# Decision thresholds that vary along the program, in a list schedule that is made at build time

## The chip, the cores and the metric

One core of one Trainium2 chip. The metric is the device time of one execution in microseconds (us). PE is TensorE, ACT ScalarE, DVE VectorE, POOL GpSimd, SP the engine that issues most DMAs. "Before" and "after" are the two kernels. A profile's span is some 1.5 to 2 us shorter than the device time of the same execution.

## The reference

```python
# x: 2048 tokens x 512, bf16; 32 heads of 16; F = 1376
def reference(x, wqkv, wo, w1, b1, w2, b2):
    xn = layernorm(x)
    # A: q, k, v = split(xn @ wqkv); p = softmax(q @ k.T * 16 ** -0.5); A = (p @ v) @ wo
    # B: a token mixer: h = layernorm(xn); u = gelu(h.T @ w1 + b1); B = (u @ w2 + b2).T
    return x + A + B
```

The cost is the softmax: 32 heads of 2048 x 2048 scores have to go through an exponential.

## The kernel before

The work is cut into 1024 score tiles of 128 x 1024, each made by two matmuls and kept in one of three PSUM slots. Its exponential is taken in one of two ways: on ACT, with one instruction; or on DVE, as integer arithmetic on the bits of a bf16 number, with three shifted copies on DVE or POOL that PE then sums up. A tile on ACT gives one PV item (four matmuls) to PE, a tile on DVE four.

The program holds no loop on the chip. At build time a scheduler in the kernel's own Python keeps a clock for each engine, asks again and again which job could start first, and appends that job to its engine's list. Six thresholds steer the choices:

```python
SEG = 8
RULES = (            # D_LATE, D_BACK, D_STEAL, PAIR_WAIT, piece_min, LATE_BY
    (0.5, 0.5, 0.3, 0.0, 6, 0),
    (0.3, 0.5, 0.3, 0.0, 6, 0),
    (0.8, 0.5, 0.3, 0.0, 4, 0),
    (0.5, 0.8, 0.3, 0.0, 6, 0),
    (0.5, 0.5, 0.45, 0.15, 6, 0),
    (0.5, 0.5, 0.15, 0.0, 4, 0),
    (0.5, 0.35, 0.3, 0.3, 4, 0),
    (0.8, 0.8, 0.3, 0.0, 99, 0),
    (0.5, 0.5, 0.3, 0.0, 4, 6),
    (0.5, 0.8, 0.45, 0.1, 4, -6),
)
RULE_OF = "000...0"                       # 128 digits, all 0
...
while True:                               # next_n: the score tile to come, 32 to 1023
    D_LATE, D_BACK, D_STEAL, PAIR_WAIT, piece_min, LATE_BY = RULES[int(RULE_OF[min(next_n, NN - 1) // SEG])]
    ...
    # may DVE take tile n?
        if qi == 0 and len(ready_q) == 1:
            if act_free - t < D_STEAL:    # ACT is about to take it
                continue
        if backlog(t) > D_BACK:           # DVE has too much waiting
            continue
    ...
    # PE: which job; is other work so late that it goes first; when are scores wanted; wait to pair two?
    jobs.append((max(t_c, est(...)), 1 if late > -LATE_BY else 3, "ext", cur_ext, 0.214))
    ...
    wants.append(sc.free["dve"] + backlog(sc.free["dve"]) + D_LATE)
    ...
    go = max(e_s, t2 if t2 <= need + PAIR_WAIT else need)
    ...
    # (piece_min: how many steps of other work must be left to place one, in four pieces, beside scores)
```

PE works in two layouts that alternate. A score phase has matmuls on 32 rows each ("S": one tile on half the array, two tiles on all of it; a piece of other work can fill a free quarter). A column phase has matmuls on 32 columns each ("C": PV items and steps of projections and of the mixer, the "other work"). The instructions that the argument touches:

```python
e.matmul(bank(bk), lhsT=KT[32*r:32*r+32, T, 128*kt:128*(kt+1)], rhs=QT[32*r:32*r+32, b % 4, :], ...)       # L776 scores
e.activation(buf(pbuf[n]), ps[:, s_*1024:(s_+1)*1024], ACTF.Exp, scale=LN2_128)                            # L800 exponential on ACT
e.tensor_scalar(buf_i(w), ps[:, s_*1024:(s_+1)*1024], IBIAS, 0.0, ALU.add, ALU.max)                        # L811 exponential on DVE
e.int64_add(buf_i(o)...)  /  e.tensor_scalar(buf_i(o), buf_i(w), float(SHIFTS[k]), 1.0, ALU.add, ALU.mult) # L817 POOL / L820 DVE: a shift
e.matmul(bank(PV_BANK)[32*c:32*c+32, 256*par:256*par+256], lhsT=vt[:, off:off+32], rhs=buf(p, ...), ...)    # L843 PV
e.matmul(bank(EX_BANK)..., tile_position=(0, 32*c)) / (..., tile_position=(32*r, 0))                        # L874 / L882 other work: step / piece
```

The softmax here doesn't subtract the row's maximum and nothing guards it: scores larger than these inputs give would overflow.

## Time and profile before

| | before |
|---|---|
| time, median of 4 runs | 689.69 us (689.63 to 689.81) |
| span of the profile | 688.0 us |
| exponentials on ACT / on DVE | 712 / 312 |
| shifts on POOL / on DVE | 643 / 293 |
| shortest spacing of ACT's exponentials | 0.903 us |
| score phases on PE (from 45 us) | 655 |

The counts come from the page's groups, which show an instruction's shape and number; where one kind has several groups (tile names pT and x_sb) they are added. The spacing and the phases are read from the start times in the trace.

### The profile page before, as it was taken

The page shows a single profiled execution, that of the slowest core. Times are in us where ns is not written, and L with a number is a line of the kernel's source. Part 1 is how long each engine was busy: PE and PEld are TensorE (multiplying, and loading weights), DVE is VectorE, ACT ScalarE, POOL GpSimd, SP SyncE. Part 2 cuts the span into 40 slices and gives each one's busy share as a digit, 9 for nine tenths or more (in the row PEclk, how much of TensorE's full clock was granted, in tenths as well). Part 3 has the DMA queues.
Part 4 walks back from the last instruction along what each step waited for, and adds up shares of the span by engine and source line. Part 5 has one row for each costly group of instructions (what it writes and reads, how often), then busy time and mean ns, then how long its engine had stood idle before and what let it go on. Part 6 is the DMA issues. An engine that isn't in the chain of part 4 may idle for free.

```text
span 688.0 us, 29503 instructions
## 1 busy us (share of the span) xinstructions
PE 674.2 (98%) x12966; PEld 310.9 (45%) x12966; DVE 620.9 (90%) x893; ACT 669.4 (97%) x732; POOL 407.9 (59%) x702
## 2 busy tenths in 40 slices
PE   8999999999999999999999999999999999999998
PEld 4534554445544454444444444444444444444444
DVE  7989899988899989999999999999999889889986
ACT  6999999999999999999999999999999999999994
POOL 5546557555566545766476576765666566555652
PEclk9999999999999999999999999999999999999999
DMA  7502100221002200122220112222221222212121
GB/s 215 132 7 52 27 16 19 51 46 25 20 19 51 47 20 20 32 44 44 52 42 21 40 46 56 53 56 55 49 60 25 57 54 56 62 42 65 40 50 44
DMA packets 86256, 32.85 MB, mean 48 GB/s; under 512 B 67440, under 2 KB 86128, under 8 KB 86128
## 3 DMA queue, kind: packets, MB, share of 16 engines
q1 hardware_dynamic: 85696, 30.58, 19.0%
q8 instruction: 101, 1.65, 1.0%
q10 hardware_dynamic: 432, 0.39, 0.2%
q14 instruction: 27, 0.22, 0.1%
HBM read 21.76 MB, written 2.35 MB: 35 GB/s over the span
## 4 chain that ended last, share of the span: by engine, by line
PE 60%; ACT 34%; DVE 3%; issue 1%; POOL 1%; DMA 0%; DVEq 0%
PE ps L843 25%; ACT pT L800 23%; PE ps L776 22%; PE ps L874 11%; ACT x_sb L800 10%; PE ps L928 1%; ACT gT_sb L985 1%; DVE pT L811 1%; DVE hx L588 1%; POOL mv L584 0%; DVE OT L1062 0%; DMA x_sb<-in_A_x_dram 0%; PE ps L669 0%; DVE x_sb L811 0%; PE ps L600 0%
## 5 line engine op out<-in xcount | busy, mean ns | idle before, releaser
L800 ACT ACTIVATE pT<-ps 128x1024 bf16<-128x1024 f32 x513 | 502.6, 1122 | 2.8 <-PE ps L776 2.1
L811 DVE TENSOR_SCALAR pT<-ps 128x1024 int16<-128x1024 f32 x229 | 279.6, 1221 | 22.7 <-PE ps L776 16.2
L776 PE MATMUL ps<-QT,KT 32*128 32x512 bf16 x2048 | 284.2, 384 | 6.3 <-ACT pT L800 2.6
L817 POOL INT64_ADD pT<-pT x339 | 205.0, 613 | 115.9 <-DVE pT L820 68.3
L843 PE MATMUL ps<-pT,V 128*32 128x256 bf16 x4732 | 245.4, 275 | 1.8 <-DVE OT L1062 1.3
L800 ACT ACTIVATE x_sb<-ps 128x1024 bf16<-128x1024 f32 x199 | 213.9, 1130 | 0.3 <-PE ps L776 0.2
L776 PEld LDWEIGHTS ps<-QT,KT 32*128 32x128 bf16 x2048 | 78.2, 91 | 183.2 <-ACT pT L800 71.9
L843 PEld LDWEIGHTS ps<-pT,V 128*32 128x32 bf16 x4732 | 111.7, 96 | 74.8 <-issue 59.3
L817 POOL INT64_ADD x_sb<-pT x135 | 82.2, 612 | 68.0 <-DVE pT L820 32.0
L843 PE MATMUL ps<-x_sb,V 128*32 128x256 bf16 x1860 | 117.8, 275 | 0.0
L811 DVE TENSOR_SCALAR x_sb<-ps 128x1024 int16<-128x1024 f32 x83 | 101.4, 1221 | 9.2 <-PE ps L776 6.6
L817 POOL INT64_ADD pT<-x_sb x118 | 71.4, 614 | 43.3 <-DVE pT L820 21.9
L820 DVE TENSOR_SCALAR pT<-pT 128x1024 int16<-128x1024 int16 x149 | 63.1, 427 | 4.4
L843 PE MATMUL ps<-pT,VM 128*32 128x256 bf16 x896 | 63.0, 275 | 0.0
L874 PE MATMUL ps<-gT_sb,wblk 128*32 128x512 bf16 (+1 forms) x704 | 60.2, 383 | 0.0
L843 PEld LDWEIGHTS ps<-x_sb,V 128*32 128x32 bf16 x1860 | 47.4, 96 | 27.7 <-issue 20.8
L874 PE MATMUL ps<-hx,wblk 128*32 128x512 bf16 x598 | 52.3, 383 | 0.0
L817 POOL INT64_ADD x_sb<-x_sb x51 | 31.1, 614 | 18.0 <-DVE pT L820 10.7
L882 PE MATMUL ps<-hx,wblk 32*128 32x512 bf16 (+1 forms) x92 | 35.6, 387 | 0.0
L843 PEld LDWEIGHTS ps<-pT,VM 128*32 128x32 bf16 x896 | 23.9, 96 | 12.9 <-issue 11.7
L820 DVE TENSOR_SCALAR x_sb<-pT 128x1024 int16<-128x1024 int16 x64 | 27.3, 428 | 2.0
L820 DVE TENSOR_SCALAR pT<-x_sb 128x1024 int16<-128x1024 int16 x59 | 25.2, 429 | 1.5
(107 smaller groups left out, 452.3 us busy)
## 6 DMA issues: line engine op xcount, KB each, us to landing
wblk<-in_B_w_dram SPq DMA_DIRECT2D x10, 512.0 KB, 4.2
wblk<-in_B_w_dram SPq DMA_DIRECT2D x16, 320.0 KB, 3.6
oC<-OT SPq DMA_DIRECT2D x248, 16.0 KB, 1.8
denb<-rden_scratch SPq DMA_DIRECT2D x124, 32.0 KB, 2.1
xr<-in_A_x_dram SPq DMA_DIRECT2D x16, 128.0 KB, 2.7
dcomp<-OT SPq DMA_DIRECT2D x124, 2.0 KB, 2.3
QT<-Qall SPq DMA_DIRECT2D x120, 16.0 KB, 1.8
out_dram<-osb SPq DMA_DIRECT2D x14, 128.0 KB, 1.9
```

The costliest lines, as they stand in the source:

```text
L588: return [dict(eng="dve", fn=lambda e: e.tensor_scalar(xn_sb[:, t, :], xn_sb[:, t, :], mv[:, t, 3:4], None, ALU.mult), reads=[("xn", t), ( ...
L776: specs.append(dict(eng="pe", fn=lambda e, r=r, bk=bk: e.matmul(bank(bk), lhsT=KT[32 * r:32 * r + 32, T, 128 * kt:128 * (kt + 1)], rhs=QT[ ...
L800: return [dict(eng="act", fn=lambda e: e.activation(buf(pbuf[n]), ps[:, s_ * 1024:(s_ + 1) * 1024], ACTF.Exp, scale=LN2_128), reads=[("ban ...
L811: return dict(eng="dve", fn=lambda e: e.tensor_scalar(buf_i(w), ps[:, s_ * 1024:(s_ + 1) * 1024], IBIAS, 0.0, ALU.add, ALU.max), reads=[(" ...
L817: return dict(eng=eng, fn=lambda e: e.int64_add(buf_i(o).bitcast(I64), buf_i(w).bitcast(I64), SHIFTS[k] * 0x0001000100010001), reads=[("pT ...
L820: return dict(eng=eng, fn=lambda e: e.tensor_scalar(buf_i(o), buf_i(w), float(SHIFTS[k]), 1.0, ALU.add, ALU.mult), reads=[("pT", w)], writ ...
L843: specs.append(dict(eng="pe", fn=lambda e, c=c, h=h, i=i, off=off: e.matmul(bank(PV_BANK)[32 * c:32 * c + 32, 256 * par:256 * par + 256], ...
L874: specs.append(dict(eng="pe", fn=lambda e, c=c, w=w: e.matmul(bank(EX_BANK)[32 * c:32 * c + w, :], lhsT=lhs_of(32 * c, 32 * c + w), rhs=rh ...
L882: return [dict(eng="pe", fn=lambda e: e.matmul(bank(EX_BANK)[0:dst_rows, :], lhsT=lhs_of(0, dst_rows)[rs], rhs=rhs[rs], start=begin, stop= ...
L928: return [dict(eng="pe", fn=lambda e, ct=ct, c=c: e.matmul(bank(EX_BANK)[32 * c:32 * c + 32, 128 * i:128 * (i + 1)], lhsT=xnT[:, ct, 128 * ...
L985: yield "act", [dict(eng="act", fn=lambda e, ap=ap: e.activation(ap, ap, ACTF.Gelu_apprx_tanh), reads=[("gT", f) for f in fts], writes=[(" ...
```

## The change

Its intent, as the change describes itself: let the thresholds differ along the program, with a new entry for every eight score tiles, found by a search whose replay of the lists has late DMAs and PE's clock. Of the search only its result is in the kernel.

```diff
-RULE_OF = "00000000000000000000000000000000000000000000000000000000000000000000000000000000000000000000000000000000000000000000000000000000"
+RULE_OF = "00008220310000100058660800426859400150020974970367941473943140809177076731670813606801617338009600085119008766223163090020510000"
```

## The prediction

> **What bounds the kernel now.** I read the page first, then the waits of ACT and DVE, the windows, and one timeline in detail.
>
> The page's first, second and fourth part:
>
> ```profile
> PE 674.2 (98%) x12966; PEld 310.9 (45%) x12966; DVE 620.9 (90%) x893; ACT 669.4 (97%) x732; POOL 407.9 (59%) x702
> ...
> PEclk9999999999999999999999999999999999999999
> ...
> PE 60%; ACT 34%; DVE 3%; issue 1%; POOL 1%; DMA 0%; DVEq 0%
> ```
>
> Two engines are nearly full and the chain of waits hops between them (PE 60%, ACT 34%); DMA is not on it. The clock row is full everywhere, so there is no clock to win.
>
> The waits of ACT, then of DVE:
>
> ```profile
> ACT oT L1162 <- PE ps L1155: 7.4, 1, 7.4
> ACT xnT L594 <- PE ps L600: 2.9, 3, 1.4
> ACT pT L800 <- PE ps L776: 2.1, 6, 0.5
> ...
> DVE pT L811 <- PE ps L776: 16.2, 69, 0.5
> DVE x_sb L811 <- PE ps L776: 6.6, 25, 0.5
> ```
>
> ACT's large waits are one in the tail and a few at the start; inside the stream its exponentials show 2.1 us of waiting. DVE waits 16.2 + 6.6 = 22.8 us for score tiles.
>
> The windows, cut where the table begins to act (about 45 us) and where the exponentials end (677 us):
>
> ```profile
> 0.00:45.00 45.00, 39.55 (x444) 19.93 (x444) 37.05 (x109) 38.28 (x46) 21.58 (x59) 1.00 0.50 133
> 45.00:677.00 632.00, 626.90 (x12418) 286.73 (x12420) 578.14 (x773) 630.22 (x686) 386.34 (x644) 1.00 0.18 42
> 677.00:688.00 11.00, 7.71 (x114) 4.28 (x106) 5.74 (x13) 0.95 (x2) 0.00 (x0) 1.00 0.14 48
> ```
>
> Only the middle 632 us can move; the 45 + 11 = 56 us around them are issued by code that doesn't consult the table. In the middle ACT is covered for 630.22 of 632 us and PE for 626.90.
>
> One stretch of the timeline (start, duration, instruction, count):
>
> ```profile
> 202.72 0.39 PE L776 MATMUL ps<-QT,KT 32*128 32x512 bf16 x2
> 202.73 0.39 PE L882 MATMUL ps<-hx,wblk 32*128 32x512 bf16 x1
> ...
> 203.04 0.40 PE L843 MATMUL ps<-pT,V 128*32 128x256 bf16 x8
> ...
> 203.15 1.18 ACT L800 ACTIVATE x_sb<-ps 128x1024 bf16<-128x1024 f32 x1
> ...
> 203.49 0.39 PE L776 MATMUL ps<-QT,KT 32*128 32x512 bf16 x4
> ...
> 203.81 0.40 PE L843 MATMUL ps<-pT,V 128*32 128x256 bf16 x8
> ...
> 204.07 1.18 ACT L800 ACTIVATE pT<-ps 128x1024 bf16<-128x1024 f32 x1
> ...
> 204.97 1.19 ACT L800 ACTIVATE x_sb<-ps 128x1024 bf16<-128x1024 f32 x1
> ```
>
> An exponential is recorded as 1.18 us, but the next starts 0.90 to 0.92 us later: work must be counted by starts. A score phase on PE takes 0.32 us whether it holds one score tile (two matmuls, here with one piece of other work beside them: 202.72 to 203.04) or two (four matmuls: 203.49 to 203.81). The phase between has three PV items of four matmuls: 203.04 to 203.49, 0.45 us.
>
> **What the Trainium skill says.** "Perfetto Trace Analysis", section "Per-instruction lifecycle", has the recorded window of a DVE or ACT instruction run to the acknowledged write, and calls PE's recorded end an estimate; so busy shares overstate how full these engines are. The trace agrees (1.18 recorded against 0.90 to 0.92 between starts). "ScalarE: Activation LUTs", section "What ACT_TABLE_LOAD costs", gives 186 ns + 0.833 ns an element for an ACTIVATE with immediate operands, with an overlap of 93 ns: 1039 - 93 = 946 ns between starts for 1024 elements. The trace has 903 ns at the shortest, and the trace decides. "TensorE: Matmul & The Clock Gate", Part 3, "The mechanism", says that matmuls on different row groups overlap; the equal 0.32 us for one and two score tiles agrees. "SBUF — State Buffer", section "SBUF: two separate sides", has DVE (in its two-port modes) and GpSimd exclude each other on a shared port pair; POOL's many waits for DVE's shifts (L820) fit that, though part of them is the program's own ordering.
>
> **The change part by part.** Only the string that names one of ten rules for each eight score tiles changes. No instruction kind is added; the order changes, and with it (a) which tiles go to DVE, (b) which of a tile's three shifts go to DVE or POOL, (c) how scores pair on PE. Of 128 entries the first four aren't consulted (32 tiles are issued before); of the other 124, 86 leave rule 0. Entries with a larger permitted DVE backlog (rules 3, 7, 9): 30; with scores wanted earlier for DVE (rule 1): 14; with an earlier takeover by DVE (rule 5): 5; with a later one (4, 9): 16; waiting to pair scores (4, 6, 9): 29. A mixture, with a lean to more tiles on DVE, and found by a search whose aim was the end time.
>
> ACT. The trace has 712 exponentials on ACT and 312 on DVE (of 1024). At 0.903 us between starts, 712 x 0.903 = 643 us. From the first start (11.4 us) to the last end (677.3 us) are 666 us. GELU with two table loads takes 398.13 to 406.10, about 8 us. What is left is 666 - 643 - 8 = 15 us, of which I read about 2 us in the fixed first part: some 13 us in the stream, most of it in pieces of 0.02 us. I give the search a third: **4 us**. Anything beyond that must come from exponentials leaving ACT: 0.90 us each.
>
> DVE. Between 45 and 677 us its start-to-start times add up to 632: 383 after the 311 exponentials (L811), 155 after the 292 shifts (L820), 93 for the rest. So one tile costs DVE (383 + 155)/311 = 1.73 us. The shortest spacings (1.135 and 0.342) would make it 1.135 + 0.94 x 0.342 = 1.46 us; the difference is the 22.8 us of waiting for scores, some 31 us in which a shift waits for its own exponential (1.258 against 1.131 us, 248 times), and what port and order cost. If the span shrinks by x, DVE has 538 - x us for 312 + (x - 4)/0.90 tiles:
> - x = 8: 316.4 tiles, 1.675 us each, 0.05 us less than now, or about 17 us of stalls gone;
> - x = 13.8 (2%): 322.9 tiles, 1.62 us each, about 0.10 us less, or 34 us of stalls gone, more than every recorded wait for scores.
> The first asks for less than all the recorded waits for scores; the second needs a second source, such as shifts given to POOL, which is busy only 59%.
>
> PE. In the middle it runs 655 score phases (322 of two tiles, 123 of one, 202 of one with a piece, 8 others) and 656 column phases; the score phases take 230 us and the column phases 401. A column phase takes about 0.118 us plus 0.1085 for each PV item plus 0.2165 for each step of other work; over that and 0.32 for a score phase only some 14 us of the 631 are left. A tile moved to DVE brings three more PV items, 3 x 0.1085 = 0.33 us. For x = 8 with four more tiles PE must lose 8 + 1.4 = 9.4 us: say 5 of the 14 us excess, and 4.4 from ten fewer pairs of phases (0.32 + 0.118 = 0.44 us each; 1.5% of 655). For x = 13.8 with eleven more it must lose 17 us: 5, and 27 pairs of phases, while every pairing that removes a half-empty score phase also removes a place for a piece.
>
> Sum: 4 us of ACT gaps + 4 to 5 exponentials off ACT (4 us) = 8 us.
>
> **The rivals.** First, the search overfits its model: the order fits modelled starts, and small differences on the chip turn into in-order waits. For it: both engines are so tight that 0.02 us slips are spread over the exponentials. Against: PE's longest recorded wait for ACT is 0.4 us, so the existing list's model fits well, and late DMAs were modelled in the search. Time then: 686 to 690. Second, the search finds the second source (POOL takes shifts, DVE takes ten or more tiles, PE pairs more): 672 to 676. For it: POOL's 41% of idle time, 322 paired phases out of a possible 512, and eighty-six entries to choose. Against: three engines have to give way together, and thresholds only nudge a greedy choice that already takes the earliest job. Third, the clock: gaps on PE could lower it; with PE this full I see no room for that, so no cost and no gain.
>
> **Range and chances.** The middle estimate is 689.65 - 8.2, about 681.5 us (-1.2%). The range 675.5 to 687 holds from two thirds of the second rival's gain to most of the first's loss. Faster by over 2% means under about 676: 0.13. Slower by over 2% would take 14 us of new waits in an order selected for its end time: 0.01. The rest, 0.86, lies within 2%.
>
> **What would show it.** DVE's exponentials at 314 to 320 instead of 312, ACT's at 704 to 710; the sum of ACT's gaps in the stream down from 13 to about 9 us; DVE's waits for scores well under 22.8 us; score phases about 645 instead of 655; head and tail as before; the same clock. If the count on DVE stays at 312 and the time still falls, the gain is gaps alone. I am wrong if over ten tiles move to DVE (then over 2%), if ACT gains nothing, or if POOL takes clearly more shifts than 643.

## The result, and the profile after

| | before | after |
|---|---|---|
| time, median (4 runs each) | 689.69 us | 685.26 us (684.96 to 685.32) |
| ratio, 95% interval | | 0.9935 (0.9917 to 0.9952) |
| span of the profile | 688.0 us | 683.2 us |
| exponentials on ACT / on DVE | 712 / 312 | 711 / 313 |
| shifts on POOL / on DVE | 643 / 293 | 658 / 281 |
| score phases on PE from 45 us | 655 | 652 |

Ratios here are the mean time of one kernel's fast runs over that of the other's of the same rounds, so not quite the ratio of the medians. The time fell by 4.43 us, 0.65%: within 2%, inside the range of the prediction, and about half of its middle estimate.

The page of after, the same three lines as in the prediction:

```profile
PE 671.5 (98%) x12975; PEld 312.9 (46%) x12978; DVE 617.0 (90%) x882; ACT 667.7 (98%) x731; POOL 416.7 (61%) x717
...
PEclk9999999999999999999999999999999999999999
...
PE 73%; ACT 21%; DVE 3%; issue 1%; POOL 1%; DVEq 0%
```

The shares are the same to two points of a per cent, the clock is full. On the chain that ended last PE's share rose from 60 to 73%: followed back from the end, it runs over ACT less.

The waits of ACT and then of DVE, after:

```profile
ACT oT L1162 <- PE ps L1155: 5.5, 1, 5.5
...
ACT pT L800 <- PE ps L776: 1.7, 4, 0.6
...
DVE pT L811 <- PE ps L776: 17.4, 61, 0.8
DVE x_sb L811 <- PE ps L776: 6.9, 31, 0.5
```

The one large wait of ACT, in the tail, is 1.9 us shorter. DVE waits 17.4 + 6.9 = 24.3 us for scores, more than the 22.8 us of before, not less.

The exponentials among the groups, before (out<-in, shape, number, busy, mean ns, idle before):

```profile
L800 ACT ACTIVATE pT<-ps 128x1024 bf16<-128x1024 f32 x513 | 502.6, 1122 | 2.8 <-PE ps L776 2.1
L811 DVE TENSOR_SCALAR pT<-ps 128x1024 int16<-128x1024 f32 x229 | 279.6, 1221 | 22.7 <-PE ps L776 16.2
...
L800 ACT ACTIVATE x_sb<-ps 128x1024 bf16<-128x1024 f32 x199 | 213.9, 1130 | 0.3 <-PE ps L776 0.2
...
L811 DVE TENSOR_SCALAR x_sb<-ps 128x1024 int16<-128x1024 f32 x83 | 101.4, 1221 | 9.2 <-PE ps L776 6.6
```

and after:

```profile
L800 ACT ACTIVATE pT<-ps 128x1024 bf16<-128x1024 f32 x488 | 486.4, 1136 | 2.2 <-PE ps L776 1.7
L811 DVE TENSOR_SCALAR pT<-ps 128x1024 int16<-128x1024 f32 x220 | 269.2, 1224 | 26.2 <-PE ps L776 17.4
...
L800 ACT ACTIVATE x_sb<-ps 128x1024 bf16<-128x1024 f32 x223 | 241.7, 1142 | 0.2
...
L811 DVE TENSOR_SCALAR x_sb<-ps 128x1024 int16<-128x1024 f32 x93 | 113.7, 1222 | 9.7 <-PE ps L776 6.9
```

513 + 199 = 712 became 488 + 223 = 711 on ACT. Which buffers they go to changed far more than how many there are.

The end of the stream, before. The first line is the last exponential on ACT; the last line is the DVE transpose that has to wait for the last PV item:

```profile
676.20 1.15 ACT L800 ACTIVATE x_sb<-ps 128x1024 bf16<-128x1024 f32 x1
...
678.70 0.94 PE L843 MATMUL ps<-pT,V 128*32 128x256 bf16 x28
...
679.91 0.72 DVE L1121 STREAM_TRANSPOSE denb<-ps 128x512 f32<-128x512 f32 x1 [1.64 <-PE ps L843]
```

and after:

```profile
673.32 1.16 ACT L800 ACTIVATE pT<-ps 128x1024 bf16<-128x1024 f32 x1
...
674.65 0.39 PE L843 MATMUL ps<-pT,V 128*32 128x256 bf16 x8
...
675.17 0.70 DVE L1121 STREAM_TRANSPOSE denb<-ps 128x512 f32<-128x512 f32 x1
```

Before, PE still had a run of 28 PV matmuls and others to do when ACT was done: 2.56 us from the end of the last exponential (677.35) to the transpose. After, it is 0.70 us (674.48 to 675.17). From there to the end both take 8.0 us.

So the 4.8 us of the two spans, followed along ACT:

| part | before | after | change |
|---|---|---|---|
| start of the first exponential | 11.43 | 11.06 | -0.4 |
| from there to the end of the last | 665.92 | 663.42 | -2.5 |
| from there to the transpose | 2.56 | 0.70 | -1.9 |
| from there to the end | 8.04 | 7.98 | -0.1 |

The first row isn't the table's: the head is issued alike, and the profiles of the experiments have 11.2 to 11.5 there without any order. The second row holds one exponential less (0.9 us). The spacings of more than 0.96 us between starts, from 45 us on and without the GELU stretch, add up to 7.3 us over the shortest before and 3.7 us after. Every one of them in before has a score matmul, or a piece beside it, as the thing that ended last. Against these 3.6 us, the shorter spacings added 1.2 us, and the first 45 us 0.8 us.

Along PE, from the first score matmul of tile 32, where the table first decides, to the transpose, the phases take 638.0 us before and 633.6 us after: score phases 232.2 and 231.0 us (658 and 655), column phases 405.8 and 402.7 us (658 and 655). By the spacings of the prediction (0.118 us for a column phase, 0.1085 for a PV item, 0.2165 for a step) column phases took 8.2 us longer than their contents before, and 4.9 after; phases that were over 0.1 us too long hold 4.9 and 2.8 us of this. A part of it are PE's waits for DVE to read the PV bank, before and then after:

```profile
PE ps L843 <- DVE OT L1062: 1.3, 5, 0.4
...
PE ps L843 <- DVE OT L1062: 0.2, 1, 0.2
```

Both lists became 4.4 us shorter, as the program did.

### The profile page after: what moved, and what is told of

Same layout as the page of the kernel before. It is cut to its first block, busy times and chain, and to the rows that moved or that the text cites. A ratio compares the mean times of both kernels' runs of the same rounds, so it can differ in the third digit from the quotient of the medians.

```text
span 683.2 us, 29532 instructions
## 1 busy us (share of the span) xinstructions
PE 671.5 (98%) x12975; PEld 312.9 (46%) x12978; DVE 617.0 (90%) x882; ACT 667.7 (98%) x731; POOL 416.7 (61%) x717
## 4 chain that ended last, share of the span: by engine, by line
PE 73%; ACT 21%; DVE 3%; issue 1%; POOL 1%; DVEq 0%
PE ps L843 29%; PE ps L776 27%; PE ps L874 14%; ACT pT L800 14%; ACT x_sb L800 6%; PE ps L928 2%; ACT gT_sb L985 1%; DVE hx L588 1%; DVE pT L811 1%; POOL mv L584 0%; PE ps L669 0%; DVE x_sb L811 0%; PE ps L600 0%; PE ps L1155 0%; PE ps L1142 0%
## 5 line engine op out<-in xcount | busy, mean ns | idle before, releaser
L800 ACT ACTIVATE pT<-ps 128x1024 bf16<-128x1024 f32 x488 | 486.4, 1136 | 2.2 <-PE ps L776 1.7
L811 DVE TENSOR_SCALAR pT<-ps 128x1024 int16<-128x1024 f32 x220 | 269.2, 1224 | 26.2 <-PE ps L776 17.4
L843 PE MATMUL ps<-pT,V 128*32 128x256 bf16 x4696 | 242.1, 275 | 0.9 <-POOL pT L817 0.3
L800 ACT ACTIVATE x_sb<-ps 128x1024 bf16<-128x1024 f32 x223 | 241.7, 1142 | 0.2
L811 DVE TENSOR_SCALAR x_sb<-ps 128x1024 int16<-128x1024 f32 x93 | 113.7, 1222 | 9.7 <-PE ps L776 6.9
L817 POOL INT64_ADD pT<-x_sb x152 | 91.5, 612 | 48.8 <-DVE pT L820 28.8
L843 PE MATMUL ps<-x_sb,V 128*32 128x256 bf16 x1904 | 120.8, 275 | 0.0
L817 POOL INT64_ADD x_sb<-pT x120 | 73.1, 613 | 45.0 <-DVE pT L820 26.1
L820 DVE TENSOR_SCALAR pT<-pT 128x1024 int16<-128x1024 int16 x138 | 58.3, 425 | 3.9
L817 POOL INT64_ADD x_sb<-x_sb x44 | 26.9, 614 | 18.1 <-DVE pT L820 11.7
```

Of the source, the lines that this page charges most:

```text
L800: return [dict(eng="act", fn=lambda e: e.activation(buf(pbuf[n]), ps[:, s_ * 1024:(s_ + 1) * 1024], ACTF.Exp, scale=LN2_128), reads=[("ban ...
L811: return dict(eng="dve", fn=lambda e: e.tensor_scalar(buf_i(w), ps[:, s_ * 1024:(s_ + 1) * 1024], IBIAS, 0.0, ALU.add, ALU.max), reads=[(" ...
L817: return dict(eng=eng, fn=lambda e: e.int64_add(buf_i(o).bitcast(I64), buf_i(w).bitcast(I64), SHIFTS[k] * 0x0001000100010001), reads=[("pT ...
L820: return dict(eng=eng, fn=lambda e: e.tensor_scalar(buf_i(o), buf_i(w), float(SHIFTS[k]), 1.0, ALU.add, ALU.mult), reads=[("pT", w)], writ ...
L843: specs.append(dict(eng="pe", fn=lambda e, c=c, h=h, i=i, off=off: e.matmul(bank(PV_BANK)[32 * c:32 * c + 32, 256 * par:256 * par + 256], ...
```

## The experiments

The scheduler has its own bookkeeping of when each job ends (the kernel can print it as its modelled end). It is no measurement; but it can be held against the runs. For the two known kernels it ends 4.6 us apart, where the chip has 4.4.

Theory A: the gain is a property of one exact order. Any threshold changed early sends every later choice another way, and the later entries were kept for the state which the earlier ones left. Theory B: the rules at their places, or the mixture, are better ones, each worth a little. Theory C, of my prediction: what counts is how many exponentials leave ACT.

### One entry changed

```diff
-RULE_OF = "0000822031000010...      (after)
+RULE_OF = "0000822011000010...
```

> The new table with one entry of 128 changed: entry 8 (tiles 64 to 71) names rule 1 instead of 3. Theory A (the gain belongs to the one exact order that the search accepted; every later entry was chosen for the state that the earlier ones left): the whole gain of 4.4 us is lost, and the time may well lie above before. The list's own bookkeeping, which put the two known orders 4.6 us apart where the chip has 4.4, ends 10.0 us later than with the unchanged table; A with this bookkeeping: 694 to 697 us. Theory B (the rules that the table names are better ones at their places, each entry worth a little): one entry in 86 is worth 0.05 us, so 685 to 686 us.

Measured: 696.18 us (696.10 to 696.42), 1.0096 of before (1.0079 to 1.0113): 10.9 us slower than after (from another call), and 6.5 us slower than before. This one of 128 entries loses the gain more than twice over (it was picked with the bookkeeping at hand; what a typical entry is worth was not tried), although the number of exponentials on ACT, 711, is the same as after. The end of PE's list shows where most of the loss is:

```profile
677.37 2.55 PE L874 MATMUL ps<-gT_sb,wblk 128*32 128x512 bf16 x44
...
682.89 2.56 PE L874 MATMUL ps<-gT_sb,wblk 128*32 128x512 bf16 x44 [1.66 <-DVE hx L1025]
```

Two blocks of 44 matmuls of the mixer's last two output tiles, which after has done among the PV items, are left to the end here. The last exponential ends at 677.85 us, half a microsecond after that of before, but from there to the end it is 16.3 us instead of 10.6.

### The same digits, shuffled

```diff
-RULE_OF = "0000" + (the 124 digits of after)
+RULE_OF = "0000" + (the same 124 digits in a random order)
```

> The same 124 digits of the new table in a random order. Theory B2 (the mixture of rules as such is better than rule 0 everywhere): about as fast as the new table, 685 to 687 us. Theory A (only the exact order): at or above before, 690 us or more; the list's own bookkeeping ends 3.0 us later than with rule 0 everywhere, so about 692.7 us, with fewer tiles on VectorE (309 instead of 312 or 313) and as many score phases as before.

Measured: 692.45 us (692.35 to 692.49), 1.0040 of before (1.0025 to 1.0055). In this one random order the mixture is worse than rule 0 alone: 715 exponentials on ACT, none of the gain. Theory B2 (the mixture as such is better) fails here; other random orders were not tried.

### The second half alone

```diff
-RULE_OF = (after)
+RULE_OF = "0" * 64 + (digits 64 to 127 of after)
```

> Rule 0 for the first 512 tiles, then the second half of the new table. Theory B: half of the gain stays, about 687.5 us. Theory A: none stays, at or above 690; the list's own bookkeeping ends 3.9 us later than with rule 0 everywhere: about 693.6 us, although its last exponential comes 1.9 us sooner and 314 tiles go to VectorE; the loss would lie in the work left after the last exponential.

Measured: 694.58 us (694.39 to 694.85), 1.0072 of before (1.0057 to 1.0087). Half of the table does not hold half of the gain: behind another first half it costs 4.9 us. ACT did finish early (710 exponentials, the last one over at 676.26, 1.1 us before that of before), and the same two blocks of the mixer were left behind it: 16.3 us from there to the end. Theory B falls with it.

### One rule everywhere, with more tiles on DVE

```diff
-RULE_OF = (after)
+RULE_OF = "9" * 128
```

> Rule 9 in all entries (a larger permitted backlog on VectorE, a wait to pair scores). Theory C, that of my prediction (each exponential that leaves ScalarE is worth 0.9 us): 315 tiles on VectorE instead of 312, so 2.7 us less, about 687 us. Its rival (TensorE's list is as long as ScalarE's, and a tile moved to VectorE adds three PV items of 0.11 us to it): ScalarE's last exponential does come about 2 us sooner, but PV items and projection work are left over behind it, and the end is 5 us later: about 694.7 us.

Measured: 695.55 us (695.38 to 696.01), 1.0087 of before (1.0072 to 1.0102). Three exponentials left ACT (709), and its last one ended 1.5 us sooner than in before, at 675.87. PE after that:

```profile
676.25 2.55 PE L874 MATMUL ps<-gT_sb,wblk 128*32 128x512 bf16 x44
678.63 0.60 PE L874 MATMUL ps<-wo_c,wkv_raw 128*32 128x512 bf16 x8
679.07 0.72 PE L843 MATMUL ps<-pT,V 128*32 128x256 bf16 x20
...
682.28 2.56 PE L874 MATMUL ps<-gT_sb,wblk 128*32 128x512 bf16 x44 [2.17 <-DVE hx L1025]
```

A first block, PV items, a wait of 2.17 us until DVE has read the bank, a second block. What ACT saved was given back on PE nearly five times over. Theory C falls in its plain form: an exponential that leaves ACT is worth its 0.9 us only if PE's list still ends with ACT's.

### Which engine's list sets the time

In the next six runs one kind of work of one engine is halved (ACT's exponentials, PE's PV items, DVE's exponentials) while all lists keep their order, so the results are wrong; the first use of each buffer, or of each part of a PSUM bank, stays whole. The edit on ACT; the one on DVE is alike:

```diff
-e.activation(buf(pbuf[n]), ps[:, s_ * 1024:(s_ + 1) * 1024], ACTF.Exp, scale=LN2_128)
+(lambda w: e.activation(buf(pbuf[n], 0, w), ps[:, s_ * 1024:s_ * 1024 + w],
+                        ACTF.Exp, scale=LN2_128))(exp_w(pbuf[n]))     # 512, 1024 at a buffer's first use
```

and on PE, in PV items:

```diff
+W = 256 if full else 128          # full: the first of each parity and the last of a block
-bank(PV_BANK)[32*c:32*c+32, 256*par:256*par+256], ..., rhs=buf(p, 512*i+256*h, 512*i+256*h+256)
+bank(PV_BANK)[32*c:32*c+32, 256*par:256*par+W], ..., rhs=buf(p, 512*i+256*h, 512*i+256*h+W)
```

> Wrong results on purpose: the kernel before in its own order, but after the first use of each buffer an exponential on ScalarE covers 512 of its 1024 columns, so its 0.90 us become about 0.48 and ScalarE loses some 290 us of work. Theory P (TensorE's list is by itself as long as the program): the time falls by no more than the gaps on TensorE, 10 to 15 us, to 675 to 680 us. Theory S (ScalarE alone bounds, TensorE only looks full): it falls by 40 us or more.

> The same with the new table. If the table shortened TensorE's own list (fewer phases), the lead of 4.4 us over before with the same halving stays, all of it. If it only made the engines' lists fit each other better (fewer gaps, nothing left over at the end), the lead shrinks: the orders differ by three pairs of phases, 3 x 0.44 us, less three PV items, 0.3 us, so about 1 us is left.

Measured: before 681.72 us (680.37 to 683.02), 0.9884 of the whole kernel (0.9865 to 0.9903); after 675.56 us (674.01 to 676.45), 0.9793 of before (0.9778 to 0.9807). The runs scatter with PE's clock, which was granted at 0.995 to 1.000; at nearly equal clock they are 680.4 (0.999) against 674.0 (1.000), and 682.95 (0.995, two runs) against 676.45 (0.995): a lead of 6.4 to 6.5 us. The page of before with halved exponentials, and ACT's waits:

```profile
PE 664.1 (98%) x12966; PEld 302.3 (45%) x12966; DVE 620.0 (91%) x893; ACT 445.7 (66%) x732; POOL 409.0 (60%) x702
```

```profile
ACT pT L800 <- PE ps L776: 99.6, 279, 2.0
ACT pT L800 <- PE ps L889: 47.3, 120, 0.7
ACT x_sb L800 <- PE ps L776: 39.6, 110, 0.8
ACT x_sb L800 <- PE ps L889: 21.3, 51, 0.7
```

ACT now waits 208 us for scores (or for pieces issued with them), and the program is 8 us shorter. This is theory P, if a little above its 675 to 680 us: PE's list, in this order, is by itself nearly as long as the program. And with the table it is shorter, by 6.4 us at nearly equal clock; my expectation of about 1 us, worked out from the number of phases, was wrong.

> Wrong results on purpose: the kernel before in its own order, but all PV items except the first two and the last of a block stream 128 columns instead of 256. Theory P and S together (both lists are nearly full): TensorE is relieved, ScalarE's 712 exponentials remain: 643 us of starts, 8 us GELU, 11 us head, 8 us tail, so no less than 670 us, and 672 to 680 us expected. If TensorE alone bounds: under 660 us is out of reach for ScalarE, so a time at the floor of 670 would say that ScalarE is the next bound at once.

> The same with the new table: 711 exponentials instead of 712. If the gain was ScalarE's (fewer exponentials), the lead over before with the same halving is about 0.9 us; if it was TensorE's being on time, the lead falls from 4.4 to that 0.9 us, since a relieved TensorE is on time in both.

Measured: before 687.15 us (686.04 to 688.20), 0.9963 (0.9948 to 0.9978); after 684.39 us (683.80 to 686.34), 0.9932 (0.9916 to 0.9949). PE was granted a clock of 0.990 to 1.000, which goes with a spread of over 2 us; at equal clock they are 686.04 against 684.05 (0.997) and 686.78 against 684.73 (0.995): a lead of 2.0 us. Both branches of the expectation for the new table name the same 0.9 us, so this run could not tell them apart, and 2.0 us is neither. The page of before with halved PV items, and the first of PE's waits:

```profile
PE 646.0 (94%) x12966; PEld 277.3 (40%) x12966; DVE 620.1 (90%) x893; ACT 669.2 (97%) x732; POOL 409.0 (60%) x702
```

```profile
PE ps L776 <- ACT pT L800: 9.4, 42, 0.4
PE ps L776 <- ACT x_sb L800: 3.7, 16, 0.5
```

PE now waits for ACT more than before (2.6 and 0.9 us there). From tile 32 to the transpose its column phases became 51.6 us shorter and its score phases 50.9 us longer, so nearly all that PE saved turned into waiting at score phases. ACT's stretch from the first to the last exponential is 665.85 us, where it was 665.92. But this profile is of the slowest of the four runs, and PE's clock was at half in two stretches (the columns are PE, PEld, DVE, ACT, POOL, PE's clock, DMA):

```profile
178.83:185.66 6.83, 6.83 (x146) 3.59 (x148) 4.50 (x7) 5.93 (x7) 3.83 (x7) 0.50 0.13 28
404.11:410.94 6.83, 6.83 (x92) 2.21 (x88) 5.50 (x9) 6.47 (x7) 3.95 (x7) 0.50 0.11 26
```

Around them (177 to 190 and 402 to 415 us) ACT's spacings lie 2.8 us over the shortest, in before 0.6 us; undisturbed, the stretch would thus be some 2 us shorter (an estimate from these two numbers). Outside them, the spacings over 0.96 us are 6.1 us over the shortest, in before 6.7: these gaps stayed, though PE had time. My 672 to 680 us for this run were too low, because I took ACT's gaps for PE's lack of time. What else they come from is asked next.

> Wrong results on purpose: the kernel before in its own order, but after the first use of each buffer an exponential on VectorE covers 512 of its 1024 columns (1.13 us becomes about 0.6, so VectorE loses some 160 us of work, and gives its PSUM slot back sooner). Theory V (ScalarE's remaining gaps, which halved PV items on TensorE did not close, come from slots that VectorE holds): the time falls by about those 7 us, to some 683 us. Theory O (they come from the fixed order itself: each gap ends with a score matmul that stands in TensorE's list behind work that must come first): within 2 us of before, 687.5 to 690 us.

> The same with the new table. Theory V: the lead of 4.4 us shrinks, since the new order has fewer such gaps to close (3.7 instead of 7.3 us): to about 1 us. Theory O: the lead stays at 4 to 5 us.

Measured: before 688.79 us (688.52 to 690.74), 0.9993 (0.9978 to 1.0008); after 684.76 us (684.73 to 684.82), 0.9928 (0.9912 to 0.9945). Theory V falls: nothing but 0.5 to 0.9 us came of it (spacings over 0.96 us: 5.5 us instead of 7.3), and the lead stays at 4.0 us. O's numbers are met; its mechanism, score matmuls that stand behind other work in PE's list, is what is left, and was not tested by itself. DVE in this run of before:

```profile
L818 DVE TENSOR_SCALAR pT<-ps 128x512 int16<-128x512 f32 (+1 forms) x229 | 168.6, 737 | 104.7 <-PE ps L776 103.5
```

It turned the saved time into waiting for scores, 103.5 us in this group alone, where the whole kernel has 16.2.

So none of these three engines alone sets the time. Less work on ACT, PE or DVE, in a fixed order, gives 8.0, 2.5 and 0.9 us by the medians of before. I read this as two lists, ACT's and PE's, of nearly equal length, each of which waits for the other at a few places, so that another order has to shorten both. Relieving two engines at once, or POOL, was not tried.

### A further search

Two tables of my own, found with the scheduler's bookkeeping alone: the first with the ten rules, the second with thresholds outside them as well.

```diff
-RULE_OF = (after)
+RULE_OF = "00006890536230559898665766026069451750445378178167616352404669801139052463673289724240234395789702863490858686873677628008380000"
```

> A table of my own: some 1,700 further single-entry changes to the new table, kept by the end time in the list's own bookkeeping, some worse ones allowed on the way; the ten rules unchanged. The bookkeeping ends 1.0 us sooner than with the new table, with 710 exponentials on ScalarE instead of 711. Theory A (the gain comes from the exact order, and the bookkeeping foretells it to about 1 us, as in the runs so far): 683.5 to 685 us. Theory F (the search without late DMAs and without the clock fits the bookkeeping's errors): no faster than the new table, 685 to 688 us.

Measured: 684.20 us (684.04 to 684.52, 5 runs), 0.9922 of before (0.9908 to 0.9936).

```diff
-RULES = (... 10 rules ...)
+RULES = (... 94 rules, as (0.93, 0.65, 0.3, 0.1, 3, 0) ...)
-RULE_OF = (after)
+RULE_OF = (0, 0, 0, 0, ...)       # an index for each of the 128 entries
```

> Another 2,700 changes from there, where an entry may also take thresholds outside the ten rules (94 different ones in the end). The bookkeeping ends 1.5 us sooner than with the new table, with 708 exponentials on ScalarE and 316 on VectorE. Theory A: 683 to 684.5 us, and VectorE can take three tiles more than with the new table if TensorE's order lets the end follow. Theory F: 685 to 688 us. Over 2% below before (under 676 us) would mean that the step of my prediction which allowed that was right; nothing so far speaks for it.

Measured: 684.25 us (684.04 to 684.46, 5 runs), 0.9922 (0.9909 to 0.9934). Both are correct, and with 5.4 us under before they have about 1 us more than after, though the 95% intervals of the ratios overlap. They were run at other times. Against their own runs of before (689.64 us) they gain 5.4 us, after against its own (689.69 us) 4.4. Theory F's 685 to 688 us were missed. The first differs from after in 92 of the 124 entries, so the gain isn't tied to after's one order: a very different one, found by a search, holds it too. The second has only 708 exponentials on ACT and 316 on DVE, yet its last exponential ends at 673.37 us, as in the first with 710: from the first start it is 662.0 against 662.2 us, so of the 1.8 us of the two that left all but 0.2 us came back as gaps.

All orders that I ran whole, as differences from before:

| table | bookkeeping | chip | exponentials on ACT |
|---|---|---|---|
| after | -4.6 | -4.4 | 711 |
| one entry changed | +5.4 | +6.5 | 711 |
| shuffled | +3.0 | +2.8 | 715 |
| second half | +3.9 | +4.9 | 710 |
| rule 9 everywhere | +5.0 | +5.9 | 709 |
| own, ten rules | -5.6 | -5.4 | 710 |
| own, more rules | -6.1 | -5.4 | 708 |

The bookkeeping is right to 1.1 us over a spread of 12 us. In these seven runs the number of exponentials on ACT foretells nothing.

## Why the prediction was right or wrong

**Range and chances: right.** 685.26 us lies in 675.5 to 687, and within 2%, which had 0.86. That three engines would have to give way together for 2% fits the runs: halving work of any single one, order kept, gave 1.2% at most on before's order, and two further searches stopped at 0.8%. But there was luck in the range: without the 1.9 us at the end, which the prediction had ruled out, the time would be 687.1 us and just outside it. (Its lower end, 14.2 us under before, is four fifths of the second rival's largest gain, 17.7 us, not two thirds.)

**ACT's gaps, 4 us: less than half.** The stretch of exponentials lost 1.6 us apart from the one exponential. I had called 13 us recoverable; real gaps over 0.96 us were 7.3 us, and those fell by 3.6, a half rather than a third. The rest of my 13 us was mostly steps of about 0.017 us, which grew slightly.

**Exponentials leaving ACT, 4 us: the failed step, mis-sized.** I let four to five leave; one did, 0.9 us. The step rested on DVE losing stalls, above all its waits for scores; these went from 22.8 to 24.3 us. Its premise that each is worth 0.90 us failed more deeply: three gone with rule 9, and the time was 5.9 us worse; 708 instead of 710 in my own tables, and no difference.

**"Only the middle 632 us can move": wrong.** Up to 1.9 us came from after the last exponential, where PV items had been left over. The table decides how far PE is behind ACT at that point; I took the whole end as fixed, and only its last 8.0 us are.

**PE: direction right, the path another.** I asked for ten fewer score phases and got three. Still PE's list is 4.4 us shorter in the profiles, and the program 6.4 us when ACT is taken out of the way. Three pairs of phases fewer are 1.3 us; three PV items and most of a step of other work more in the columns take 0.5 us of that back, so 0.8 us are left. The rest is less excess: 3.3 us in column phases, 2.1 of them in phases over 0.1 us too long, and 0.3 us in score phases. Why the many small ones became shorter stays open. The excess itself I had mis-added: with the prediction's own terms, from 45 to 677 us, it is 28 us and not 14. Of these, 20.5 us are in score phases, because 0.32 us is their shortest time: those of two tiles take 0.37 us in the mean.

**POOL and DVE.** Fifteen more shifts went to POOL (658), which I had named as a sign of being wrong. It gave DVE 12 shifts less and its busy time fell by 3.9 us, but DVE's time isn't what sets the end, as the halved exponentials on DVE show. That POOL's waits for DVE's shifts fit a shared port proves nothing: the scheduler itself makes each shift on POOL wait for DVE's last instruction that uses this port, and no run here takes this ordering away.

**Rivals.** The first, a search that fits its model's errors, did not come about: bookkeeping and chip agree within 0.2 us for this change. The second, 2% by a second source, did not either. The clock cost nothing in after: in its profile it drops to half at 682.0 us, when the last matmul, done at 679.9, is over. Of the runs with halved work, some lost time to it.

What I hadn't seen is how the gain is held: not by the rules that I counted, but by an order that a search has selected as a whole. The count of entries with a larger backlog, an earlier score and so on, from which I took "a lean to more tiles on DVE", did not foretell the time: the same digits in one other order are 2.8 us slower than before.

## What to carry to other kernels

When two engines' lists are both full, look at where both end and at how much work each has left when the other stops, not at busy shares: removing work from one of them buys little, and here an order that took three tiles from ACT cost nearly six microseconds. This build-time list schedule can jump with a single threshold (one entry of 128 was worth 11 us), so I would search a tuned table again after any edit, which was not tried; where its bookkeeping agrees with the chip to about a microsecond, the search is cheap. Before explaining such a change by its parameters, shuffle them: it is a run or a few, and it helps to tell a better rule from a selected order.

## What the Trainium skill lacked or had wrong

- "TensorEngine Tiling (Array Packing)", section "Key Properties", says that changing the tiling mode drains PE, without giving a cost. Here a column phase takes about 0.118 us beyond its 0.1085 us for each PV item, and a score phase at the shortest 0.32 us, whether it has two matmuls or four; no run isolates the change of mode itself.
- "ScalarE: Activation LUTs", section "What ACT_TABLE_LOAD costs": its figures give 946 ns between starts for 1024 elements (worked out in the prediction), with no separate figure for reading PSUM; the trace has 903 to 904 ns at the shortest, reading PSUM. The skill isn't without it: the overhead of about 51 ns on PSUM in "Perfetto Trace Analysis", section "Optimizing Scalar/DVE Operations", gives, with the 853 ns of the elements, an estimate of 904 ns, which the prediction didn't use. A fifth to a quarter of the spacings lie near 920 ns, a step for which I found no page. For 512 elements the first page gives 186 + 427 = 613 ns of duration; the run with halved exponentials has 597.
- "Perfetto Trace Analysis", section "Identifying the Most-Contended Engine", says to optimize the engine with the highest occupancy first, and to judge PE's headroom by the share of its weight loads (and by MFU, the share of peak arithmetic, not computed here) instead of its matmuls. That share is 45% here (PEld), which points to ACT with its 97%; but halving ACT's exponentials brought 8.0 us of 690, with PE's list nearly as long, and halving PE's PV columns 2.5 us: the page has no case of two lists that bind together.
